# Key-value product folded into the output weight with 32x32 tiles of the TensorE array

## The chip, the cores and the metric

The kernel runs on one core of a Trainium2 chip. The metric is the device time of one execution in microseconds; the time given for a kernel is the median over its runs. TensorE does the matmuls and writes to PSUM, VectorE and ScalarE work element by element and take results out of PSUM, SyncE (SP) issues most of the DMAs. Each engine works through its own queue in order.

## The reference

The whole block is linear attention followed by a token-mixing MLP, both with a pre-LayerNorm and a residual, on 2048 tokens of width 1024. The change touches the attention:

```python
def _A_ref(x, wqkv, wo):
    B, S, D = x.shape
    H = 32; Dh = D // H
    qkv = (x @ wqkv).reshape(B, S, 3, H, Dh)   # then to (3, B, H, S, Dh)
    q, k, v = qkv[0], qkv[1], qkv[2]
    phi = lambda t: jnp.where(t > 0, t + 1, jnp.exp(t)) + 1e-6
    pq, pk = phi(q), phi(k)
    kv = jnp.einsum("bhsd,bhse->bhde", pk, v)
    z = jnp.einsum("bhsd->bhd", pk)
    num = jnp.einsum("bhqd,bhde->bhqe", pq, kv)
    den = jnp.einsum("bhqd,bhd->bhq", pq, z)[..., None] + 1e-6
    o = num / den
    return o.transpose(0, 2, 1, 3).reshape(B, S, D) @ wo
```

There are 32 heads of 32 columns, so `kv` is one 32x32 matrix for each head. Since `num @ wo` is linear in `kv`, a kernel may multiply each head's `kv` into its 32 rows of `wo` first, and then multiply `pq / den` by that product.

## The kernel before

**Stages.** The attention's front end projects K and V, adds up `kv` and the sums of `pk` in PSUM (`kv_ps`, by `kv_accum`), and computes parts of Q in between (`q_fill`). Then comes the stretch that the change lies in, lines 1382 to 1582. After it the output projection runs over 16 blocks of 128 tokens (`seed`, `out_mm`, `out_evac`), and then the MLP, which takes the larger part of the time.

**The stretch around the change.** 128 partitions hold four heads, so the 1024 columns of Q, K, V are eight blocks j of four heads q (`ND` = 8, `HB` = 4, `DH` = 32).

- Lines 1384 to 1392, VectorE: `kv_ps` goes to `kvbd`, one 128x128 block-diagonal matrix for each j, in four instructions (one for each head q of a block, all j at a time). Then `zz` is made of the sums of `pk`. Three units of Q (`q_fill`) run on TensorE meanwhile.
- `kv_transpose`: eight TensorE transposes of `kvbd` into one PSUM bank, one ScalarE copy to `kvT`.
- `load_wo`: `wo` arrives in two DMAs of 1 MB on SP. Its place in SBUF, `wo_sb`, is used for sums of weights by the V projection before (`tv`), so the load waits until that is done. Behind it on SP's queue stand the first MLP weights (`load_w1`, two of 1 MB), four rows of x (`load_xr`), and then the denominators' DMAs.
- A loop of 16 steps n (lines 1567 to 1582). Each step computes one unit of Q with eight matmuls (`q_held`), taken out of PSUM by Exp and Relu on ScalarE and finished by two operations on VectorE. Steps 1 to 8 also run `fold(n - 1)`: two matmuls of 128x128 by 128x512 for block j, one result copied to `wf` (the same place as `wo_sb`, as fp16) by ScalarE, one by VectorE. Steps 0, 2 and 9 run a denominator (`den`): eight matmuls on column tiles of 32, Ln and Exp on ScalarE into `rd_sb`, and a DMA to `rd_dram`; `den_spread` brings it back to all partitions in eight DMAs of 128 KB, each to 32 partitions. `scale_q` multiplies Q by it, `first_sums` prepares MLP weights, both on VectorE.

**Order.** Nearly everything here is held in program order on its engine by `pin` (the helpers `ht`, `hs`, `hv`, `hd` do that; all their instructions carry line 230). The load of `wo` and the `kvbd` pieces are not pinned; a scheduler places them.

**Banks.** [...] `acc_tile` hands out accumulators from a ring of five (two of pool `acc`, three of pool `accx`); the denominators have three (`ndp`). A unit or a fold can start when the bank that it is given has been read out.

Of the kernel before, what the change touches and what calls it, by code (L numbers as in the profile page):

```python
# [10 lines left out]
P = 128  # L11
# [4 lines left out]
ALU = mybir.AluOpType  # L16
PSUM = bass.MemoryType.PSUM
# [4 lines left out]
DH = 32  # L22
# [8 lines left out]
def kernel(  # L31
# [12 lines left out]
    nc = tc.nc  # L44
    x = A_x.flatten_outer_dims()
    o_dram = out.flatten_outer_dims()
    S, D = x.shape
    F = B_w1.shape[1]
    NS, ND, NF = S // P, D // P, F // P
    CW = min(BANK, D)  # L50
    NDC = D // CW
# [7 lines left out]
    HB = P // DH  # L59
# [6 lines left out]
    acc = actx_psum.enter_context(tc.tile_pool(name="acc", bufs=2, space=PSUM))  # L66
    accx = ExitStack()
    acc_ring = [acc]

    def more_acc(bufs):  # L70
        pool = accx.enter_context(tc.tile_pool(name="accx", bufs=bufs, space=PSUM))
        acc_ring[:] = [acc, pool, acc, pool, pool][0:2 + bufs]

    def less_acc():
        accx.close()
# [2 lines left out]
    def acc_tile():  # L78
        acc_ring.append(acc_ring.pop(0))
        return acc_ring[-1].tile([P, BANK], F32, tag="acc", name="acc_t")  # L80

    more_acc(3)

    pin = tc.keep_in_program_order
# [56 lines left out]
    def load_w1(u, half, hold=lambda ins: ins):  # L141
        if half == 0:
            w1_tiles[u] = w_tile(wpool, WLEN)[:, 0:NS * CW].rearrange("p (k f) -> p k f", f=CW)
        k = slice(half * NSP, (half + 1) * NSP)
        hold(nc.sync.dma_start(
            w1_tiles[u][:, k, :],
            B_w1[:, u * CW:(u + 1) * CW].rearrange("(k p) f -> p k f", p=P)[:, k, :],
        ))
# [84 lines left out]
    hv, ht, hs, hd = (Held(e, True) for e in (nc.vector, nc.tensor, nc.scalar, nc.sync))  # L233
# [545 lines left out]
    with ExitStack() as actx:  # L779
# [11 lines left out]
        wo_sb = hstat.tile([P, ND, D], BF16)  # L791
        pqpool = actx.enter_context(tc.tile_pool(name="pqpool", bufs=1))
        pqT = pqpool.tile([P, ND, S], BF16)
        kvbd = pqpool.tile([P, ND, P], BF16)
# [6 lines left out]
        a2k = xctx.enter_context(tc.tile_pool(name="a2k", bufs=4))  # L801

        wqkv_v = A_wqkv.rearrange("(k p) c -> p k c", p=P)
        wo_v = A_wo.rearrange("(k p) c -> p k c", p=P)

        with ExitStack() as a1:
            a1w = a1.enter_context(tc.tile_pool(name="a1w", bufs=1))
# [474 lines left out]
            kv_ps = kvp.tile([P, ND, DH + 1], F32, name="kvps")  # L1282
# [98 lines left out]
                q_fill()  # L1381
            nc.vector.memset(zz[:, :, 0:3 * HB], 0.0)
            nc.vector.memset(zz[:, :, 3 * HB:], float(S))
            for q in range(HB):
                own = slice(q * DH, (q + 1) * DH)
                nc.vector.tensor_scalar(kvbd[own, :, own], kv_ps[own, :, 0:DH], 1.0 / S, None, ALU.mult)
            nc.vector.tensor_tensor(
                zz[:, :, HB:2 * HB],
                kv_ps[:, :, DH:DH + 1].to_broadcast([P, ND, HB]),
# [1 line left out]
                ALU.mult,  # L1391
            )

        more_acc(3)
        warmctx.close()
        kvT = xctx.enter_context(tc.tile_pool(name="kvtpool", bufs=1)).tile([P, ND, P], FP16, name="kvT")
        wpool = sactx.enter_context(tc.tile_pool(name="wpool", bufs=2, side="right"))
        pools["sa"] = mctx.enter_context(tc.tile_pool(name="sapool1", bufs=4, side="right"))

        def load_wo(c):  # L1400
            nc.sync.dma_start(wo_sb[:, :, c * CW:(c + 1) * CW], wo_v[:, :, c * CW:(c + 1) * CW])

        pools["i5"] = mctx.enter_context(tc.tile_pool(name="is0", bufs=1, side="right"))
        pools["is_bufs"] = 4
        a3p = actx.enter_context(ExitStack())
        ndp = a3p.enter_context(tc.tile_pool(name="ndp", bufs=3, space=PSUM))
        rd_dram = [dram.tile([P, SW], FP16, name=f"rd_dram{u}") for u in range(NSC)]

        with ExitStack() as a3:

            def kv_transpose():
                tp = acc_tile()[:].bitcast(BF16).rearrange("p (j f) -> p j f", f=P)
                for j in range(ND):
                    ht.transpose(tp[:, j, :], kvbd[:, j, :], ident[:])
                hs.copy(kvT[:], tp)

            wf = wo_sb[:].bitcast(FP16)

            def fold(j):
                for c in range(NDC):  # L1420
                    cols = slice(c * CW, (c + 1) * CW)
                    ps = acc_tile()
                    ht.matmul(ps[:, 0:CW], lhsT=kvT[:, j, :], rhs=wo_sb[:, j, cols], start=True, stop=True)
                    (hs.copy if c == 0 else hv.tensor_copy)(wf[:, j, cols], ps[:, 0:CW])

            rdbs = {}
            SPREAD = (0, 2, 1, 3)
# [23 lines left out]
            def den_spread(u):  # L1451
                rows = rd_dram[u].rearrange("(g o h) n -> o h g n", g=4, h=HB)
                for h in range(2):
                    rdb = thirds[(2 * SPREAD.index(u) + h) % 3].bitcast(FP16).rearrange("p (j n) -> p j n", n=SW)
                    for q in range(HB):
                        hd.dma_start(
                            rdb[q * DH:(q + 1) * DH, :, :],
                            rows[h, q].unsqueeze(0).to_broadcast([DH, 4, SW]),
                        )
                    rdbs[u, h] = rdb  # L1460

            def den(u):
                den_inv(u, den_mm(u))

            def scale_q(u, h):
                v = pqT[:, h * NH:(h + 1) * NH, u * SW:(u + 1) * SW]
                hv.tensor_tensor(v, v, rdbs.pop((u, h)), ALU.mult)

            def q_held(u, j):
                qp = acc_tile()  # L1470
                for kt in range(ND):
                    ht.matmul(
                        qp[:, 0:SW],
                        lhsT=wq_sb[:, kt, j * P:(j + 1) * P],
                        rhs=xnT[:, kt, u * SW:(u + 1) * SW],
                        start=(kt == 0),
                        stop=(kt == ND - 1),
                    )
                phi_evac(pqT[:, j, u * SW:(u + 1) * SW], qp[:, 0:SW], SW, a2k)
# [14 lines left out]
            def seed(i):  # L1494
                if i < NS:
                    xr = xrs.pop(i)
                    seeds[i] = [acc_tile() for dc in range(NDC)]
                    for dc in range(NDC):
                        hs.copy(seeds[i][dc][:, 0:CW], xr[:, dc * CW:(dc + 1) * CW])
# [40 lines left out]
            def combine_h(q):  # L1540
                combine(hE[:, q, :], hO[:, q, :], hT2[:, q, :], hT3[:, q, :], hT4[:, q, :], hv)

            for c in range(NDC):
                load_wo(c)
            for half in range(2):
                load_w1(0, half, pin)
            for i in range(XRL + 1):
# [2 lines left out]
            def first_sums():  # L1550
                cur = Quad([Mixer1(0), Mixer1(1)])
                for m in (5, 6, 7, 3):
                    yield pin(cur.asums(m))
                cur.in5 = Inner(cur.sts, 5, None, "i5", cur.sink5, cur.sum5)
                Held.on = True
                cur.in5.sums()
                Held.on = False
                yield cur

            for _ in range(2):  # L1560
                acc_ring.append(acc_ring.pop(0))
            sums_at, ahead = (4, 8, 9, 11, 13), first_sums()
            scale_at = {5: (0, 0), 6: (0, 1), 10: (2, 0), 12: (2, 1), 15: (1, 0)}
            den_at = {0: 0, 2: 2, 9: 1}
            spread_at = {0: 0, 6: 2, 12: 1}
            kv_transpose()
            for n, (u, j) in enumerate(q_units[8:]):
                if n == len(q_units) - 8 - 1:
                    seed(0)
                q_held(u, j)  # L1570
                if 1 <= n < 1 + ND:
                    fold(n - 1)
                if n in den_at:
                    den(den_at[n])
                if n in spread_at:
                    den_spread(spread_at[n])
                if n in (12, 13):
                    load_w1(1, n % 2, pin)
                if n in scale_at:
                    scale_q(*scale_at[n])  # L1580
                if n in sums_at:
                    cur = next(ahead)
# [254 lines left out]
```

## Time and profile before

| what | value |
|---|---|
| median of 3 runs | 557.93 us (557.29 to 558.2) |
| the profiled execution | 557.03 us, its span 555.3 us |
| granted TensorE clock | 1.00 throughout |
| fold matmuls (`acc_t<-wo_sb,kvT`) | 16, first at 145.8 us, last at 162.3 us |
| the two DMAs of `wo` | issued at 133.6 and 134.1 us, 5.2 and 7.6 us to landing |
| four `kvbd` pieces on VectorE | from 137.0 us, 0.40 to 0.43 us each |
| transposes of `kvbd` on TensorE | from 141.3 us |
| copies of the folds | eight on ScalarE (0.59 us), eight on VectorE (0.68 us) |
| stretch from the transposes to the end of the 16 units | 141.3 to about 179 us |

Times of single instructions are counted in microseconds from the start of the span. An instruction's length is not its cost: matmuls are pipelined, so a row of eight matmuls of 379 ns each takes 8 x 0.216 us. What counts is the distance from the start of one to the start of the next. A line of the timeline gives the start, the length, the engine, the line of code, the operation with output and inputs, and how often it stands there in a row.

### The profile page before, as it was taken

The numbers are of one execution on the slowest core, as the hardware profiler recorded it, in microseconds if no ns is written. First come the engines' busy times: TensorE is split into PE (matmuls) and PEld (weight loads), VectorE is DVE, ScalarE is ACT, GpSimd is POOL, SyncE is SP. The second block draws the span as 40 slices with busy tenths as digits, with TensorE's granted clock in tenths as the row PEclk, the third lists the DMA queues.
The fourth block names the chain that finished last, engine by engine and source line by source line (L and its number), as shares of the span: only waits on it lengthen the run. The fifth ranks groups of instructions, "written<-read, shape, count | busy, mean of one in ns | idle before, by whom it ended". The sixth has DMA issues, their size and how long they took to land.

```text
span 555.3 us, 9676 instructions
## 1 busy us (share of the span) xinstructions
PE 548.3 (99%) x3754; PEld 316.7 (57%) x3771; DVE 443.6 (80%) x851; ACT 289.0 (52%) x614; POOL 26.2 (5%) x36
## 2 busy tenths in 40 slices
PE   8999999999999999999999999999999999999997
PEld 3444446644444444456666766666444667767665
DVE  7798888755497788889989789887896878749747
ACT  5747678766776877645546465564210412413311
POOL 1000000000000000000000000000003103103111
PEclk9999999999999999999999999999999999999999
DMA  8933341202867951203140440413869649849434
GB/s 295 312 77 77 84 89 20 40 1 97 293 161 209 317 176 76 77 1 109 44 152 15 138 148 6 152 43 90 208 200 238 198 129 244 207 135 237 94 107 75
DMA packets 83934, 74.56 MB, mean 134 GB/s; under 512 B 15650, under 2 KB 76336, under 8 KB 83888
## 3 DMA queue, kind: packets, MB, share of 16 engines
q1 hardware_dynamic: 79504, 69.87, 42.0%
q0 software_dynamic: 4096, 3.68, 4.9%
q8 instruction: 29, 0.48, 0.3%
q10 hardware_dynamic: 288, 0.39, 0.2%
q14 instruction: 17, 0.14, 0.1%
HBM read 59.12 MB, written 11.67 MB: 127 GB/s over the span
## 4 chain that ended last, share of the span: by engine, by line
PE 95%; DMA 2%; ACT 1%; DVE 1%; issue 1%; ACTq 0%; DVEq 0%
PE psI L230 25%; PE psC L230 16%; PE acc_t L230 14%; PE psB L230 8%; PE psC L970 4%; PE psB L970 4%; PE psA L970 4%; PE acc_t L890 3%; PE acc_t L1299 2%; PE psB L342 2%; PE psA L342 2%; PE psE L970 2%; PE psC L342 2%; PE psA L230 1%; PE psE L342 1%; DMA rd_dram<-shared_sb 1%
## 5 line engine op out<-in xcount | busy, mean ns | idle before, releaser
L230 PEld LDWEIGHTS <-is 128*128 128x128 f16 x736 | 71.8, 98 | 31.2 <-DVE hi L230 0.4
L230 PEld LDWEIGHTS <-sa 128*128 128x128 f16 x606 | 59.2, 98 | 27.1
L230 PEld LDWEIGHTS <-wq 128*128 128x128 bf16 (+1 forms) x496 | 48.5, 98 | 28.2 <-issue 1.0
L230 PE MATMUL acc_t<-wo_sb,pqT 128*128 128x512 f16 x256 | 55.6, 379 | 0.0
L487 POOL DMA_DIRECT2D out_dram<-wq x28 | 24.3, 927 | 517.2 <-ACT wq L490 486.9
L230 PEld LDWEIGHTS <-pqT 128*128 128x128 bf16 x256 | 25.0, 98 | 30.5 <-issue 0.6
L230 DVE TENSOR_TENSOR t<-psI,t 128x256 f32<-128x256 f32 (+1 forms) x45 | 20.8, 475 | 22.2 <-PE psI L230 20.9
L190 DVE TENSOR_SCALAR e_sb<-e_sb 128x512 bf16<-128x512 bf16 x64 | 18.4, 288 | 19.7 <-ACT e_sb L185 19.6
L230 PE MATMUL psC<-gs,wq 128*128 128x512 f16 x140 | 34.1, 379 | 0.0
L970 PEld LDWEIGHTS <-xs 128*128 128x128 f16 x208 | 19.7, 98 | 22.3 <-DVE xs L959 0.8
L230 PE MATMUL psC<-hT,sa 128*128 128x512 f16 x112 | 31.2, 379 | 0.0
L230 PE MATMUL psI<-hi,is 128*128 128x256 f16 x200 | 30.0, 273 | 0.0
L230 PE MATMUL psB<-hT,sa 128*128 128x512 f16 x112 | 29.7, 379 | 0.0
L230 PE MATMUL acc_t<-xnT,wq_sb 128*128 128x512 bf16 x125 | 29.3, 379 | 0.3
L230 DVE BATCH_NORM_STATS2 hst<-acc_t 128x6 f32<-128x512 f32 x32 | 21.4, 692 | 9.0 <-ACT h_bf L230 8.9
L185 ACT ACTIVATE e_sb<-acc_t 128x512 bf16<-128x512 f32 x32 | 19.1, 598 | 18.1 <-PE acc_t L1299 9.5
L970 PE MATMUL psA<-wkv,xnT 128*128 128x512 bf16 x96 | 25.9, 379 | 0.4
L970 PEld LDWEIGHTS <-xnT 128*128 128x128 bf16 x156 | 15.2, 98 | 18.7 <-issue 1.1
L230 PE MATMUL psC<-hT,wq 128*128 128x512 f16 x96 | 24.6, 379 | 0.0
L230 ACT CAST h_bf<-acc_t 128x512 bf16<-128x512 f32 x32 | 18.4, 582 | 11.9 <-PE acc_t L230 11.8
L230 DVE TENSOR_TENSOR e<-psI,es 128x256 f32<-128x256 f32 x20 | 8.5, 425 | 19.9 <-PE psI L230 19.9
L230 ACT COPY psI<-psI 128x256 f32<-128x256 f32 x50 | 18.0, 360 | 11.6 <-PE psI L230 9.8
(245 smaller groups left out, 1123.5 us busy)
## 6 DMA issues: line engine op xcount, KB each, us to landing
wq<-in_B_w_dram SPq DMA_DIRECT2D x14, 1024.0 KB, 7.8
wq<-in_B_w_dram SPq DMA_DIRECT2D x12, 896.0 KB, 7.4
gs<-parked SPq DMA_DIRECT2D x9, 896.0 KB, 4.7
shared_sb<-rd_dram SPq DMA_DIRECT2D x32, 128.0 KB, 3.8
out_dram<-h_bf SPq DMA_DIRECT2D x16, 256.0 KB, 2.0
x_sb<-in_A_x_dram SPq DMA_DIRECT2D x14, 256.0 KB, 3.0
w2o<-in_B_w_dram SPq DMA_DIRECT2D x4, 896.0 KB, 11.3
out_dram<-wq POOLq DMA_DIRECT2D x28, 128.0 KB, 4.8
```

The source lines that it names most:

```text
L185: pin(nc.scalar.activation(e_sb[:], src, ACT.Exp))
L190: pin(nc.vector.tensor_scalar(e_sb[:], e_sb[:], 1.0, PHI_EPS, ALU.min, ALU.add))
L230: return (lambda *a, **kw: pin(op(*a, **kw))) if self.always or getattr(Held, self.key) else op
L342: pe.matmul(ps[:, cols], lhsT=lhs[:, k, :], rhs=mv(k)[:, cols], start=(start and k == 0), stop=(k == self.nk - 1), skip_group_check=True,)
L487: nc.gpsimd.dma_start(to, ot[:, a:b], accum_op=ALU.add)
L890: mm = nc.tensor.matmul(pp[:, 0:CW], lhsT=xnT[:, kt, i * P:(i + 1) * P], rhs=wkv[:, kt, c * CW:(c + 1) * CW], start=(kt == 0), stop=(kt == ...
L970: pin(nc.tensor.matmul(ps[:], lhsT=lhs[:, k, :], rhs=rhs[:, k, :], start=(start and k == 0), stop=(k == hk2 - 1), skip_group_check=True,))
L1299: nc.tensor.matmul(qp[:, 0:SW], lhsT=wq_sb[:, kt, j * P:(j + 1) * P], rhs=xnT[:, kt, u * SW:(u + 1) * SW], start=(kt == 0), stop=(kt == ND ...
```

## The change

The product of `kv` and `wo` is computed head by head on 32x32 tiles of the array. A block-diagonal 128x128 matrix would use only the four tiles on the diagonal. So the four blocks of one half (j = 4a + b, b = 0 to 3) are turned against each other: head q of block b sits in rows r = (q + b) mod 4 of its 32-row groups, both in `kvbd` (as columns, before the transposes) and in `wo_sb` (as partitions). Then the 16 heads of the half occupy 16 different tiles (r, q), and a group of 16 matmuls of 32x32 by 32x512 does four blocks for one half of the columns. Tile (r, q) writes partitions of q in the bank of block b.

There are four such groups (two halves by two column halves), in steps 1, 3, 5 and 7, each with two ScalarE and two VectorE copies. `load_wo` becomes 16 DMAs of 128 KB, each to 32 partitions; the `kvbd` pieces become 16. The ring has six banks (four in `accx`) in another order, and the denominators keep two.

```diff
     def more_acc(bufs):
         pool = accx.enter_context(tc.tile_pool(name="accx", bufs=bufs, space=PSUM))
-        acc_ring[:] = [acc, pool, acc, pool, pool][0:2 + bufs]
+        acc_ring[:] = [acc, pool, acc, pool, pool] if bufs == 3 else [pool, pool, pool, acc, acc, pool]
...
-        wo_v = A_wo.rearrange("(k p) c -> p k c", p=P)
+        wo_v = A_wo.rearrange("(a b q e) c -> e a b q c", b=HB, q=HB, e=DH)
+
+        def row_of(q, j):
+            return (q + j) % HB
...
+            turned = kvbd[:].rearrange("p (a b) (r e) -> p a b r e", b=HB, e=DH)
+            sums_v = kv_ps[:, :, 0:DH].rearrange("p (a b) e -> p a b e", b=HB)
             for q in range(HB):
                 own = slice(q * DH, (q + 1) * DH)
-                nc.vector.tensor_scalar(kvbd[own, :, own], kv_ps[own, :, 0:DH], 1.0 / S, None, ALU.mult)
+                for b in range(HB):
+                    nc.vector.tensor_scalar(turned[own, :, b, row_of(q, b), :], sums_v[own, :, b, :], 1.0 / S, None, ALU.mult)
...
-        more_acc(3)
+        more_acc(4)
...
-        def load_wo(c):
-            nc.sync.dma_start(wo_sb[:, :, c * CW:(c + 1) * CW], wo_v[:, :, c * CW:(c + 1) * CW])
+        def load_wo():
+            to = wo_sb[:].rearrange("p (a b) c -> p a b c", b=HB)
+            for q in range(HB):
+                for b in range(HB):
+                    r = row_of(q, b) * DH
+                    nc.sync.dma_start(to[r:r + DH, :, b, :], wo_v[:, :, b, q, :])
...
-        ndp = a3p.enter_context(tc.tile_pool(name="ndp", bufs=3, space=PSUM))
+        ndp = a3p.enter_context(tc.tile_pool(name="ndp", bufs=2, space=PSUM))
...
-            def fold(j):
-                for c in range(NDC):
-                    cols = slice(c * CW, (c + 1) * CW)
-                    ps = acc_tile()
-                    ht.matmul(ps[:, 0:CW], lhsT=kvT[:, j, :], rhs=wo_sb[:, j, cols], start=True, stop=True)
-                    (hs.copy if c == 0 else hv.tensor_copy)(wf[:, j, cols], ps[:, 0:CW])
+            def fold(n):
+                a, c = divmod(n, NDC)
+                cols = slice(c * CW, (c + 1) * CW)
+                ps = [acc_tile() for _ in range(HB)]
+                for r in range(HB):
+                    rows = slice(r * DH, (r + 1) * DH)
+                    for q in range(HB):
+                        b = (r - q) % HB
+                        j, own = a * HB + b, slice(q * DH, (q + 1) * DH)
+                        ht.matmul(
+                            ps[b][own, 0:CW], lhsT=kvT[rows, j, own], rhs=wo_sb[rows, j, cols],
+                            start=True, stop=True, skip_group_check=True, tile_position=(r * DH, q * DH),
+                        )
+                for b in range(HB):
+                    (hs.copy if b % 2 == 0 else hv.tensor_copy)(wf[:, a * HB + b, cols], ps[b][:, 0:CW])
...
-            for c in range(NDC):
-                load_wo(c)
+            load_wo()
...
-            for _ in range(2):
-                acc_ring.append(acc_ring.pop(0))
...
+            fold_at = {1: 0, 3: 1, 5: 2, 7: 3}
...
-                if 1 <= n < 1 + ND:
-                    fold(n - 1)
+                if n in fold_at:
+                    fold(fold_at[n])
```

## The prediction

> **What bounds the kernel now.** First the page's engine table and the engine shares of the chain that ended last:
>
> ```profile
> PE 548.3 (99%) x3754; PEld 316.7 (57%) x3771; DVE 443.6 (80%) x851; ACT 289.0 (52%) x614; POOL 26.2 (5%) x36
> ...
> PE 95%; DMA 2%; ACT 1%; DVE 1%; issue 1%; ACTq 0%; DVEq 0%
> ```
>
> TensorE works almost without a hole, so a matmul saved is time saved, provided that nothing else ends last at that place. The exception is the DMA's 2%. I looked for it in the chain in order of time (start, length, what) around the change:
>
> ```profile
> 144.72 0.57 ACT den_ps L230
> 145.29 0.02 issue
> 145.31 0.61 ACT shared_sb L230
> 145.92 0.02 issue
> 145.94 5.75 DMA rd_dram<-shared_sb
> ...
> 152.26 0.59 ACT e_sb L185
> 152.85 0.49 ACT r_sb L187
> 153.34 0.49 ACT wo_sb L230
> 153.83 0.04 issue
> 153.87 1.24 PE acc_t L230 x5
> ```
>
> ScalarE's Exp of the denominator (`den_inv`) writes `rd_sb`, which a DMA carries to DRAM. That DMA takes 5.75 us and lands at 151.7. The next denominator's Exp needs the same `rd_sb`, so ScalarE, which works in order, stands until 151.7; everything queued behind it (Exp and Relu of unit n=3, then copies of `fold`) is late. What this does to TensorE is in its timeline (start, length, operation; a record is missing here and there):
>
> ```profile
> 135.48 0.67 PE L920 MATMUL kvps<-vaug,pk 128*32 128x33 bf16 x64
> 136.07 5.35 PE L1299 MATMUL acc_t<-xnT,wq_sb 128*128 128x512 bf16 x23
> ...
> 143.53 0.61 PE L230 MATMUL den_ps<-pqT,zz 128*32 128x512 bf16 x8
> 144.08 1.90 PE L230 MATMUL acc_t<-xnT,wq_sb 128*128 128x512 bf16 x7
> ...
> 150.78 0.59 PE L230 MATMUL acc_t<-wo_sb,kvT 128*128 128x512 bf16 x2
> 151.22 1.89 PE L230 MATMUL acc_t<-xnT,wq_sb 128*128 128x512 bf16 x8
> 152.94 0.82 PE L230 MATMUL acc_t<-wo_sb,kvT 128*128 128x512 bf16 x2
> 153.87 1.89 PE L230 MATMUL acc_t<-xnT,wq_sb 128*128 128x512 bf16 x7
> ```
>
> A fold of one j (two matmuls) takes 150.78 to 151.22, 0.44 us; the one at 152.94 takes 0.93. So TensorE loses 0.49 us to that DMA. Why the DMA is slow: it stands behind the 2 MB of `wo`, 2 MB of `w1` and 1 MB of x on one queue. The last fence has the queue's issues, then the load in stretches of 2 us (busy time of PE, PEld, DVE, ACT, POOL, then granted clock, DMA share, GB/s):
>
> ```profile
> 133.63 1.01 SPq L1401 DMA_DIRECT2D wo_sb<-in_A_wo_dram  x2
> ...
> 151.70 3.65 SPq L230 DMA_DIRECT2D shared_sb<-rd_dram  x8
> ```
> ```profile
> 136.00:138.00 2.00, 1.95 (x25) 0.94 (x15) 1.56 (x5) 0.67 (x2) 0.00 (x0) 1.00 1.04 363
> 138.00:140.00 2.00, 2.00 (x11) 0.91 (x10) 1.56 (x5) 1.35 (x3) 0.00 (x0) 1.00 1.08 384
> 140.00:142.00 2.00, 2.00 (x17) 1.18 (x16) 0.72 (x2) 1.36 (x4) 0.00 (x0) 1.00 1.08 381
> ...
> 156.00:158.00 2.00, 2.00 (x11) 0.92 (x10) 1.90 (x4) 1.41 (x4) 0.00 (x0) 1.00 1.00 227
> ```
>
> With 128 partitions at a time the DMA moves 363 to 384 GB/s. In the last line it carries `shared_sb<-rd_dram`, 128 KB to 32 partitions each, and at a full share it moves only 227.
>
> **The folds on the array.** Sixteen matmuls of 512 columns leave, 8 x 0.43 = 3.46 us. Four groups of sixteen 32x32 matmuls come. The trace has no row tiles; the nearest row is the denominator, eight matmuls on four column tiles. From the end of the unit before it (its last matmul starts at 143.22, plus 0.22) to 144.08 it takes 0.64 us for two rounds of four, so one round costs 0.64 - 0.22 = 0.42, the change of tiling on both sides included. A group of 16 that runs in one round has 12 more starts, at 9 ns as in the kvps row (64 in 0.59 us) at most: 0.42 to 0.53, I take 0.50. Four groups: 2.0, a saving of 1.46 us. The other bound: rows of the array take turns, four rounds, 0.42 + 3 x 0.22 and the starts, 1.1 us a group. The outermost: sixteen turns, 0.42 + 15 x 0.22 = 3.7 us. I take one round, since four tiles with four moving operands already overlap in this row.
>
> [...]
>
> **The weight's load.** Two DMAs of 1 MB become sixteen of 128 KB, each to 32 partitions. In the order of the changed program three go first, as soon as the V run's matmuls that read blocks 0, 1, 4, 5 of `wo_sb` are done (the last starts at 129.99, so about 130.4), while the DMA is idle; the other 13 follow from about 133.2. Issue on SP: eight spreads take 3.65 us, 0.46 each, so 13 end at 139.2; behind them stand two `w1` loads, four x rows (0.43 each), done near 142, and the `rd_dram` write, which is not ready before 145.94. The longer issue is hidden by 4 us. Data: now 2.1 MB run from 134.5; summing the stretches, they are through at 140.8. Then 13 x 131 KB = 1.70 MB at 227 GB/s need 7.5 us from 134.4, to 141.9: everything behind on the queue is 1.1 us later. Bound below: if only issue limits, the last is issued at 139.2 and through at 140.4, 0.4 us earlier than now. I take +1.1, because the spread has the same size and the same 32 partitions. Its packets are smaller and its source is one row read 32 times, so the lower end is a real possibility.
>
> [...]
>
> The folds themselves do not wait for `wo`: the first stands at 145.8, landing near 143, cover 2.8 us.
>
> **The wait that decides.** With six banks in the order of the ring, unit n=5 reuses the bank of n=3 (four of six go to each fold). Exp and Relu of n=3 stand behind the blocked Exp. So n=5 can start 1.7 us after the landing (151.7 to the end of Relu, 153.34, and a little). Now n=5 starts at 153.87. Landing now 151.7, after the change 151.7 + 1.1 = 152.8: n=5 starts at 154.5, 0.6 later than now. Without any wait TensorE would come there at 153.87 - 0.49 - 4 x 0.43 + 2 x 0.50 = 152.65, so 1.85 us of standing replace 0.49; the saving of the first two groups is swallowed whole. The last two groups keep theirs: 2 x 0.50 against 4 x 0.43, -0.73. Sum -0.1.
>
> **VectorE.** The four `kvbd` pieces (0.42 us each, 256 elements) become 16 of 64 elements. `zz` has 32 elements and 0.19 us; between the two 0.22 each, 3.6 us instead of 1.7, from 137.04 to 140.6, and 0.7 us of phi operations that the new order puts between them: 141.3. The transposes on TensorE wait for them and start at 141.26, so the 2.5 us of cover are just used up; 0 to 0.2 us late, hidden before n=5 by the 1.85. Bound: 0.42 each gives 144.1, 2.9 us late, and then n=5 starts at 155.5, 1.0 later still, 558.8. Casts out of PSUM stay eight and eight on ScalarE and VectorE, two and two at a time; the second group's last VectorE cast ends some 3.4 us after the landing and the third group starts 3.4 after it (1.7 plus a unit of 1.73), no cover left: +0.1. The denominators' buffers go from three to two; the third denominator comes 18 us after the first's Exp, so nothing.
>
> **Sum.** 0.6 - 0.73 + 0.1 = 0.0; the load's price has more room below (to -0.4) than above, so I write -0.1. It is made against the profiled execution, 557.03 us with a span of 555.3 and 1.7 around it; the median, 557.93, lies 0.9 above, and I carry the difference over to it: 557.8. About 0.2%, 1.1 us, is what a measurement of this kernel can tell from no change.
>
> **The rivals.**
> 1. The weight arrives as fast as it is issued (DMA -0.4). Landing 151.3, n=5 at 153.0: -0.87 - 0.73 = -1.6, 556.3. For it: in 154 to 156 the same spreads still ran at 239 GB/s while partly waiting for issue. Against: 227 at a full share.
> 2. Slower: rows of the array take turns in each group, 1.1 us instead of 0.50. The first two groups still fit ahead of 154.5 (152.65 + 1.2 = 153.85); the last two cost 2.2 against 1.73. 0.6 + 0.47 + 0.1 = +1.2, 559.1; it decides from about 1.05 us a group. Against it: the overlapping denominator; for it: nothing in the trace uses row tiles. This is also the case in which the change does not do what it says.
> 3. The queue is later still: at the longest landing of such a spread, 6.4 us, with eight in flight, 0.8 us each, 13 x 0.8 = 10.4, the landing comes 4.0 later than now, +3.4 from n=5 on, 560.6 in all.
>
> **Chances.** Forecast 0.42 (its own range 556.9 to 558.8), rival 1 0.30, rival 2 0.21, rival 3 0.07. Faster by over 0.2% is rival 1 and an edge of the forecast, 0.32; slower is most of 2, all of 3 and an edge, 0.29; the rest, 0.39, within. The range 555.9 to 559.8 holds rival 1 with its spread and rival 2, and leaves out rival 3 and the edges.
>
> **What would show it.** In the changed profile: a group's 16 matmuls from start to the next unit near 0.5 us (1.1: rival 2); DMA rate 134 to 142 near 220 GB/s or near 280 (rival 1); landing of the first `rd_dram` write near 152.8; TensorE's gap ahead of n=5 near 1.8 us and none elsewhere; the transposes at 141.3. I am wrong if that gap is absent, or if TensorE waits for `kvbd` or for the weight.

## The result, and the profile after

| | before | after |
|---|---|---|
| median, 17 runs each | 557.53 us (556.79 to 558.83) | 561.67 us (557.53 to 565.59) |
| profiled execution, its span | 557.03, 555.3 us | 562.1, 560.2 us |

The ratio, estimated from all runs and not the quotient of the two medians, is 1.0065, with an interval of 1.0046 to 1.0085: slower, and above the range of the prediction. The clearest hint on the page of the changed kernel is its engine table and the engine shares of the chain that ended last:

```profile
PE 550.2 (98%) x3819; PEld 315.6 (56%) x3819; DVE 444.7 (79%) x863; ACT 288.9 (52%) x614; POOL 26.3 (5%) x36
...
PE 91%; DMA 5%; DVE 2%; ACT 1%; SPq 1%; issue 0%; DVEq 0%; ACTq 0%
```

The DMA's share grew from 2% to 5% and VectorE's from 1% to 2%; TensorE's busy time grew too, by 1.9 us, though matmul work was taken out. The first question is where the 4.9 us of span lie. Starts of the same matmuls in both traces give it:

| from, to | before | after | more |
|---|---|---|---|
| span's start to the first fold | 145.82 | 146.06 | 0.24 |
| first fold to first matmul of the output projection | 29.52 | 31.89 | 2.37 |
| to the first `psI<-gi,is` of the second MLP stage | 254.54 | 254.54 | 0 |
| that to TensorE's last matmul | 121.90 | 124.09 | 2.19 |
| to the end | 3.49 | 3.62 | 0.13 |

So there are two places, and the second is 300 us behind the edit. First the changed stretch. The chain in order of time:

```profile
144.30 1.85 PE acc_t L230 x8
...
146.78 7.21 DMA rd_dram<-shared_sb
...
154.58 0.59 ACT e_sb L185
155.17 0.50 ACT r_sb L187
...
155.71 4.35 PE acc_t L230 x26
```

It is the same wait as before, with 7.21 us instead of 5.75, and issued later: it lands at 154.00, 2.3 us after the old 151.69. ScalarE stands for it:

```profile
154.08 0.60 ACT L230 ACTIVATE shared_sb<-den_ps 128x512 f16<-128x512 f32 x1 [4.07 <-DMA rd_dram<-shared_sb]
```

TensorE's timeline shows what hangs on it (in brackets the idle time ahead and who ended it):

```profile
141.42 0.61 PE L230 MATMUL acc_t<-ident,kvbd 128*128 128x128 bf16 x8
...
146.06 0.43 PE L230 MATMUL acc_t<-wo_sb,kvT 32*32 32x512 bf16 x16
146.43 1.90 PE L230 MATMUL acc_t<-xnT,wq_sb 128*128 128x512 bf16 x8
...
151.01 1.90 PE L230 MATMUL acc_t<-xnT,wq_sb 128*128 128x512 bf16 x8
155.71 3.45 PE L230 MATMUL acc_t<-xnT,wq_sb 128*128 128x512 bf16 x8 [2.80 <-ACT r_sb L187]
159.09 0.43 PE L230 MATMUL acc_t<-wo_sb,kvT 32*32 32x512 bf16 x16
```

Sixteen small matmuls take 0.37 us to the next unit, 146.06 to 146.43. The unit at 155.71 (n=5) waits 2.80 us, and then takes 3.4 us where its neighbours take 1.8. The stretches of 2 us explain both (busy time of PE, PEld, DVE, ACT, POOL, then granted clock, DMA share, GB/s):

```profile
134.00:136.00 2.00, 2.00 (x58) 0.95 (x57) 0.43 (x1) 0.86 (x2) 0.00 (x0) 1.00 0.43 132
136.00:138.00 2.00, 2.00 (x43) 1.03 (x34) 1.43 (x8) 0.82 (x2) 0.00 (x0) 1.00 0.47 140
138.00:140.00 2.00, 2.00 (x11) 0.94 (x10) 1.90 (x12) 1.19 (x3) 0.00 (x0) 1.00 0.93 257
...
154.00:156.00 2.00, 0.29 (x1) 0.10 (x1) 0.60 (x2) 1.92 (x5) 0.00 (x0) 0.87 0.27 61
156.00:158.00 2.00, 2.00 (x6) 0.73 (x5) 1.86 (x6) 1.62 (x4) 0.00 (x0) 0.50 0.85 238
158.00:160.00 2.00, 2.00 (x22) 0.59 (x21) 1.39 (x3) 0.81 (x2) 0.00 (x0) 0.78 0.93 221
```

Between 134 and 138 the weight moves at 132 to 140 GB/s with the DMA engines under half busy; before, the line of 136 to 138 had 363. And from 155.5 to 158.9 the granted clock is 0.50. The drop falls into the gap, and it costs another 1.6 us: from n=5 to the next start are 3.38 us, where 146.43 to 148.26 is 1.83. That the gap is its cause is tested below. Last, the queue of SP (start, time to the last issue's end):

```profile
130.12 11.10 SPq L1411 DMA_DIRECT2D wo_sb<-in_A_wo_dram  x16
141.42 1.03 SPq L145 DMA_DIRECT2D wq<-in_B_w_dram  x2
142.49 4.19 SPq L230 DMA_DIRECT2D shared_sb<-in_A_x_dram  x4
146.78 0.36 SPq L230 DMA_DIRECT2D rd_dram<-shared_sb  x1
```

The sixteen issues end at 141.2, the x rows at 146.7. ScalarE has the denominator's Exp done at 146.07, so now the write waits 0.7 us for its turn, where before the x rows were issued 2.7 us ahead of it. What the write stands behind is late as well: the last x row landed at 153.69, 0.3 us ahead of it, and before at 151.32, 0.4 us ahead. So its landing follows the data ahead of it, more than its own turn. Before, w1 and the x rows stood on the queue like this:

```profile
136.27 2.84 SPq L145 DMA_DIRECT2D wq<-in_B_w_dram  x2
139.16 4.06 SPq L230 DMA_DIRECT2D shared_sb<-in_A_x_dram  x4
```

The second place is in the MLP. VectorE's rows of both kernels (the kernel before first), then TensorE's of the changed one:

```profile
469.56 0.62 DVE L230 TENSOR_TENSOR is<-wq 128x896 f16<-128x896 bf16 x1
```
```profile
474.40 0.63 DVE L230 TENSOR_TENSOR is<-wq 128x896 f16<-128x896 bf16 x1 [2.15 <-DMA wq<-in_B_w_dram]
```
```profile
475.75 0.94 PE L230 MATMUL psI<-gi,is 128*128 128x256 f16 x7 [1.62 <-DVE is L230]
```

VectorE stands 2.15 us for a load of `w2` (896 KB to `wq`). It was issued at 463.4; fifteen of its sixteen parts had landed by 471.3, the last one came at 474.4, 3 us behind the others. Before, the same load was issued at 460.8, landed at 469.2, and was wanted at 469.56: 0.36 us of cover. I call this the pause.

### The profile page after: what moved, and what is told of

Read it like the earlier page. It is cut to its first block, busy times and chain, and to the rows that moved or that the text cites. A ratio compares the mean times of both kernels' runs of the same rounds, so it can differ in the third digit from the quotient of the medians.

```text
span 560.2 us, 9816 instructions
## 1 busy us (share of the span) xinstructions
PE 550.2 (98%) x3819; PEld 315.6 (56%) x3819; DVE 444.7 (79%) x863; ACT 288.9 (52%) x614; POOL 26.3 (5%) x36
## 4 chain that ended last, share of the span: by engine, by line
PE 91%; DMA 5%; DVE 2%; ACT 1%; SPq 1%; issue 0%; DVEq 0%; ACTq 0%
PE psI L230 23%; PE acc_t L230 15%; PE psC L230 14%; PE psB L230 8%; PE psC L973 4%; PE psB L973 4%; PE psA L973 4%; PE acc_t L893 3%; PE acc_t L1302 2%; PE psA L342 2%; PE psB L342 2%; PE psE L973 2%; DMA wq<-in_B_w_dram 2%; PE psC L342 2%; DMA wkv<-in_A_wqkv_dram 1%; DMA rd_dram<-shared_sb 1%
## 5 line engine op out<-in xcount | busy, mean ns | idle before, releaser
L230 PE MATMUL acc_t<-xnT,wq_sb 128*128 128x512 bf16 x128 | 30.7, 394 | 2.8 <-ACT r_sb L187 2.8
```

Source lines behind the costliest of these rows:

```text
L230: return (lambda *a, **kw: pin(op(*a, **kw))) if self.always or getattr(Held, self.key) else op
```

## The experiments

All are compared with the kernel before on the same chip (557.7 to 558.0 us). Medians are of 6 to 12 runs, the other two columns of one execution each. They are "fold to output" (29.52 before, 31.89 after) and "MLP" (121.90 and 124.09), the two rows of the table above that moved most.

| kernel | median us | ratio, interval | fold to output | MLP |
|---|---|---|---|---|
| after, `wo` in two DMAs | 557.86 | 1.0002, 0.9989 to 1.0014 | 28.34 | 123.97 |
| before, `wo` in sixteen | 563.39 | 1.0096, 1.0078 to 1.0114 | 33.54 | 123.65 |
| after, second buffer | 558.53 | 1.0000, 0.9981 to 1.0019 | 27.37 | 123.95 |
| after, gap filled | 559.57 | 1.0026, 1.0016 to 1.0036 | 30.81 | 121.90 |
| after, seven DMAs | 557.62 | 0.9986, 0.9971 to 1.0002 | 27.37 | 121.90 |
| after, seven, second buffer | 556.85 | 0.9966, 0.9953 to 0.9980 | 27.37 | 123.62 |
| the same once more | 557.48 | 0.9975, 0.9959 to 0.9992 | 27.37 | 124.28 |
| before, second buffer | 557.23 | 0.9989, 0.9979 to 0.9998 | 29.03 | 122.84 |
| before, shifted | 560.13 | 1.0039, 1.0025 to 1.0053 | 29.57 | 123.98 |
| before, shifted, flat start | 560.07 | 1.0035, 1.0020 to 1.0049 | 29.64 | 123.76 |
| after, seven, buffer, shifted | 558.42 | 1.0010, 0.9999 to 1.0020 | 27.37 | 122.72 |
| the same, flat start | 557.56 | 0.9990, 0.9979 to 1.0001 | 27.37 | 122.60 |

**Is it the load? (two runs)** First the changed kernel with the load of before. It leaves out the turning of `wo`, so its product takes wrong rows, and it stands here for its times alone:

```diff
-            for q in range(HB):
-                for b in range(HB):
-                    r = row_of(q, b) * DH
-                    nc.sync.dma_start(to[r:r + DH, :, b, :], wo_v[:, :, b, q, :])
+            for c in range(NDC):
+                nc.sync.dma_start(wo_sb[:, :, c * CW:(c + 1) * CW], wo_v[:, :, c * CW:(c + 1) * CW])
```

> The changed kernel, but wo loaded as before (two DMAs of 1 MB, rows not turned, so the product takes the wrong rows of wo). Theory A (the sixteen DMAs to 32 partitions delay the rd_dram write behind them; TensorE stands about 3 us ahead of unit n=5 and its clock is then halved for 3.4 us): the write lands near 151.7 instead of 154.0, the gap ahead of n=5 falls from 3.0 to about 0.8 us, granted clock 1.00, and the groups' saving comes through: 556.2, 1.3 below the kernel before. Rival B (the tile groups, six banks or sixteen kvbd pieces cost the time): stays near 561.

Its chain, then its TensorE:

```profile
145.76 5.92 DMA rd_dram<-shared_sb
```
```profile
153.40 1.89 PE L230 MATMUL acc_t<-xnT,wq_sb 128*128 128x512 bf16 x8 [0.82 <-ACT r_sb L187]
```

The landing is back at 151.7, the gap is 0.82 us, and the clock stays at 1.00 there. Fold to output is 1.18 us shorter than before. Yet the median is 557.86: the MLP row took 2.1 us back, in a pause at 509.9 in this profile.

Then the kernel before with sixteen DMAs to 32 partitions each, rows not turned, everything else old (the loop above, with `r = q * DH`):

> The kernel before, with nothing changed but the load of wo in sixteen DMAs of 128 KB to 32 partitions (rows in their old places). Theory A: the rd_dram write lands near 154, TensorE stands 2.3 us longer than before and the clock drops as in the changed kernel: 557.5 + 2.3 + 1.7 = 561.5. Rival B: the load alone costs nothing, 557.5.

Its chain and its TensorE, then its clock (second number from the right is the DMA share, before it the clock):

```profile
146.81 8.01 DMA rd_dram<-shared_sb
```
```profile
156.53 0.58 PE L230 MATMUL acc_t<-wo_sb,kvT 128*128 128x512 bf16 x1 [2.67 <-ACT r_sb L187]
```
```profile
158.00:160.00 2.00, 1.78 (x6) 0.65 (x5) 2.00 (x3) 0.43 (x1) 0.00 (x0) 0.52 0.83 223
```

The load alone, with the old folds, gives the late landing (154.82), the gap, the halved clock and 4.0 us more from fold to output. Of the 5.7 us by which the median grew, another 1.7 lie in the MLP row. Turning the rows is not needed for it, and the small tiles are not either.

**Is it the one buffer, and is it the clock? (two runs)** A second `rd` tile for u == 2 leaves the load late but lets nobody wait for it:

```diff
-                hs.activation(rd_sb, ps[:], ACT.Exp, scale=-1.0)
-                hd.dma_start(rd_dram[u][:], rd_sb)
+                rd = rd_two[:] if u == 2 else rd_sb
+                hs.activation(rd, ps[:], ACT.Exp, scale=-1.0)
+                hd.dma_start(rd_dram[u][:], rd)
```

> The changed kernel with a second buffer for the denominator of n=2, so that its Exp needn't wait for the first rd_dram write. Theory A: no gap ahead of n=5, clock 1.00, whole saving of the groups (1.7) and the 0.5 that the kernel before loses there: 555.6. Rival C (without that wait the next one takes its place: VectorE's casts or the second write): between 556.5 and 558. Rival B: near 561.

TensorE runs through the place (the third group at 154.36 instead of 159.09):

```profile
150.80 3.63 PE L230 MATMUL acc_t<-xnT,wq_sb 128*128 128x512 bf16 x15
154.36 0.43 PE L230 MATMUL acc_t<-wo_sb,kvT 32*32 32x512 bf16 x16
```

Fold to output is 27.37, 4.52 less than in the changed kernel. The lowest run, 555.25, is near the 555.6 that was expected of the kernel; the median, 558.53, is not, and the MLP row is 2.05 longer than before.

The next one leaves the wait and gives TensorE idle work in it, whose result nobody reads:

```diff
+                if n == 5:
+                    idle = ndp.tile([P, SW], F32, tag="den", name="den_ps")
+                    for t in range(14):
+                        ht.matmul(idle[:], lhsT=wq_sb[:, 0, 0:P], rhs=xnT[:, 0, 0:SW], start=True, stop=True)
```

> The changed kernel with 14 idle matmuls (3.0 us, into a free denominator bank) ahead of unit n=5, where TensorE stands. The wait stays, the idling goes. Theory A: n=5 starts where it did (155.7), its eight matmuls take 1.7 us instead of 3.5, clock 1.00, 1.7 below the changed kernel: 560.0. Rival D (the slow matmuls after the gap are not caused by idling): no gain or, with the 3 us of matmuls, a loss: 561.7 or more.

```profile
152.56 3.19 PE L230 MATMUL den_ps<-xnT,wq_sb 128*128 128x512 bf16 x14
156.00 1.89 PE L230 MATMUL acc_t<-xnT,wq_sb 128*128 128x512 bf16 x8 [0.25 <-ACT r_sb L187]
```
```profile
156.00:158.00 2.00, 2.00 (x24) 0.81 (x23) 1.87 (x5) 1.98 (x5) 0.00 (x0) 1.00 0.72 207
```

Unit n=5 starts even later (156.00), but takes 1.89 us instead of 3.45, at a granted clock of 1.00 instead of 0.50. Fold to output becomes 1.08 us shorter by useless work. That separates the two costs: the wait, and the clock that the wait costs. It holds beyond the profiles: the mean clock is 0.997 or less in 14 of 17 executions of the changed kernel and in 4 of 6 of the kernel before with sixteen DMAs, and 0.999 or more in all 12 with the gap filled. The two of those six that kept their clock took 561.4 us, the other four 563.3 or more. The median falls by 2.1; the other half of that is not shown to come from the clock, since in this profile the MLP row has no pause either.

**A load that is turned but wide.** A block b only has to be turned by 32 b partitions, so it takes one DMA for b = 0 and two for each other, seven in all:

```diff
+            for b in range(HB):
+                at = b * DH
+                nc.sync.dma_start(to[at:P, :, b, :], wo_v[0:P - at, :, b, :])
+                if b:
+                    nc.sync.dma_start(to[0:at, :, b, :], wo_v[P - at:P, :, b, :])
```

> The changed kernel with wo in seven wider DMAs (block 0 of each half to all 128 partitions, the turned blocks in pieces of 96+32, 64+64 and 32+96 partitions; the same bytes to the same places as the sixteen). Theory A (it is the sixteen DMAs to 32 partitions that make the denominator's DMA late): wo is through near 141.5, the first rd_dram write lands at 151.7 to 152.5 instead of 154.0, TensorE stands 0.8 to 1.5 us ahead of unit n=5 and its clock is not lowered there. Without a pause in the MLP's second stage that gives 556.3; with the pauses that the kernel with two DMAs showed (557.86), 558.0. Rival (what counts is that a turned load can't run at full rate at all): landing 153 or later, the clock lowered, 560.5 or more.

SP's queue, then TensorE:

```profile
136.69 1.01 SPq L145 DMA_DIRECT2D wq<-in_B_w_dram  x2
137.75 4.44 SPq L230 DMA_DIRECT2D shared_sb<-in_A_x_dram  x4
145.79 0.33 SPq L230 DMA_DIRECT2D rd_dram<-shared_sb  x1
150.66 3.94 SPq L230 DMA_DIRECT2D shared_sb<-rd_dram  x8
```
```profile
150.71 3.63 PE L230 MATMUL acc_t<-xnT,wq_sb 128*128 128x512 bf16 x15
154.26 0.43 PE L230 MATMUL acc_t<-wo_sb,kvT 32*32 32x512 bf16 x16
```

The spread that waits for the write is issued at 150.66: the landing is 1.0 us earlier than in the kernel before, probably because three of the seven, half of the bytes, go from 129.8 while the DMA is idle (of the sixteen, three carried 384 KB by then). No gap is left, even with the one buffer. The rival, that a turned load must be slow, falls. The profiled run, which has no pause, takes 555.06 us; the median, 557.62, again lies higher.

> The changed kernel with the seven wider DMAs and a second buffer for the second denominator, so that neither the landing nor the Exp can stop TensorE. No gap ahead of n=5, clock 1.00. Front part as in the run with the second buffer alone. If the pause of the MLP's second stage (VectorE waiting for a w2 load) comes as often as there: 558.4, with single runs at 555.3; if the pause had to do with the narrow load: 555.5.

> The changed kernel with seven wider DMAs and the second buffer, once more, beside its shifted copy: 556.9, lowest 555.05, if the earlier 12 runs speak for it; up to 558.4 if they were lucky.

Two sets of 12 runs, medians 556.85 and 557.48, lowest 555.05 and 555.08: this is the fastest version, 0.25 to 0.34% below the kernel before. That the second buffer adds to it is not shown: fold to output is 27.37 with it and without, and the intervals of the three ratios overlap.

**The old wait.** The second buffer in the kernel before:

> The kernel before with a second buffer for the second denominator, so that its Exp waits for no DMA. It measures the old wait alone: TensorE's instructions do not move against each other, so the fetches fall as before. Prediction's reading (0.49 us): 557.2 to 557.3 against 557.7, the fold at 152.94 followed after 0.44 us instead of 0.93.

Fold to output falls from 29.52 to 29.03, by 0.49 us, the time from 558.0 to 557.23.

**The pause.** In the runs that have no long gap (two DMAs, second buffer, seven DMAs) some executions come out as the stretch says (555.1 to 556.1) and most some 2 us higher. What could the edit change at 470 us? The trace has a DMA queue of the kind `instruction` in pieces of 16 KB, about 1 us each, one every 12 to 28 us, 29 before and 30 after. I take it for the queue that fetches TensorE's instructions; by the pages that would be 63 bytes before and 64 after for each of the 7525 and 7638 matmuls and weight loads, an estimate from the two counts, and no run shows whose they are. The change has 96 TensorE instructions more (64 matmuls with their weight loads instead of 16), so if it is, all later fetches fall at other places. I moved them on purpose, in both directions, with small matmuls at the start:

```diff
             warm_up(1, ln[0][6][:])
+            for t in range(48):
+                pin(nc.tensor.matmul(warm_tiles[t % 5][0:2, 0:2], lhsT=warm[:, 0:2], rhs=warm[:, 0:2], start=True, stop=True))
```

(80 in the changed kernel with seven DMAs and the second buffer.)

> The kernel before with 48 matmuls of two columns added to TensorE's idle time near 6 us: 96 instructions, as many as the change adds. Theory F: its fetches move to where the changed kernel has them, VectorE waits for a w2 load once or twice between 465 and 515 us in most runs, median 559.3, lowest 557. Rival (the pause has another cause): 557.7, as the kernel before.

> The kernel with seven DMAs and the second buffer, and 80 matmuls of two columns added to TensorE's idle time near 6 us (160 instructions with their weight loads). Theory F: TensorE's instructions come in DMAs of 16 KB, and the changed kernel has 96 more of them, so that such a fetch now falls at 457 to 462 us, 1.5 us before a w2 load is issued, and delays one DMA engine's share of it, where before it fell at 468.4, after the load. 160 more move the fetches to near the old places: no pause of VectorE for wq between 465 and 515, median 555.6. Rival (the pause does not depend on where fetches fall): as the kernel without the 80, near 558.4.

These cost something at the start (the first fold came 0.9 us late in the one, 2.2 in the other, where the clock was lowered for 3.4 us near 8 us). So I repeated both with part of the warming-up matmuls left out in exchange:

> The kernel before with TensorE's instruction count raised by 96, as the change raises it, but without the 0.95 us that the 48 small matmuls cost at the start: 51 of two columns stand among the warming-up matmuls, three of which (512 columns) are left out in exchange. K and V projections start within 0.2 us of the kernel before. Theory F (where the 16 KB instruction fetches fall decides how often a w2 load comes too late): the single runs stand 1.5 to 2.5 us above the lowest of the kernel before, median 558.9, with a fetch near 460 and the pause of VectorE for wq near 470. Rival (the start's delay made the difference): 557.8, as the kernel before.

> The changed kernel with seven wider DMAs, the second buffer, and 160 more TensorE instructions, 85 matmuls of two columns among the warming-up matmuls in exchange for five of those, so that the start is no later and the fetches fall where the kernel before has them (469 and 507). Theory F: median 1.0 us above its lowest, as in the kernel before: 556.1, below the kernel without the shift. Rival: the same as that kernel, 556.9 or, if the pauses are as in the run with sixteen DMAs, 558.4.

The starts weren't flat: 0.85 and 1.6 us later than in the profiles of the unshifted kernels (of which others start up to 1.0 late by themselves). Hence the medians missed their numbers. The MLP rows do not depend on the start. Sorted by where a fetch falls against the issue of the first of the two critical `w2` loads (the second follows 39 to 42 us later):

| fetch falls | kernels | MLP, us over 121.90 |
|---|---|---|
| 1.2 to 1.7 us ahead of the load | after; second buffer; two DMAs; seven; seven with buffer, twice; before shifted, twice | 2.2; 2.1; 2.1; 0.0; 1.7; 2.4; 2.1; 1.9 |
| 4.9 us ahead | gap filled | 0.0 |
| 7.4 to 8.1 us behind | before; before with buffer; seven with buffer shifted, twice | 0.0; 0.9; 0.8; 0.7 |
| 7.4 behind, and 2.7 behind the second load | before, sixteen DMAs | 1.8 |

VectorE's row in the shifted kernel before (flat start), with the old folds and the old load:

```profile
472.42 0.63 DVE L234 TENSOR_TENSOR is<-wq 128x896 f16<-128x896 bf16 x1 [1.82 <-DMA wq<-in_B_w_dram]
```

Shown: with 96 more instructions the kernel before has the pause in both profiles and lost 2.1 us, of which at most 0.9 lies at the start; with 160 more, the pause of the kernel with seven DMAs and the second buffer went from 1.7 and 2.4 us to 0.8 and 0.7. Not shown: that the fetch itself holds up the load. A fetch takes about 1 us, and the late part of the load came 3 us after the others; its last packets run beside the output's writes from POOL's queue (`out_dram<-wq`), two of which, landing at 472.92 and 473.91, had one late part too, 0.8 and 1.1 us behind the other fifteen. It is one profile for each kernel, seven DMAs ran without a pause at the bad place, with two DMAs the pause came at the second load, and the kernel before with sixteen DMAs has a pause of 1.7 us with no TensorE instruction added. An earlier start of the load, the direct cure, was not tried.

TensorE itself does not show a late fetch: among its listed waits (0.2 us and more) in the profiles of before, after, two DMAs, sixteen in the kernel before, second buffer and gap filled, those of the MLP, up to 1.62 us, end with VectorE or ScalarE. Whether a fetch can hold up another engine's tightly timed load is what stays open here.

## Why the prediction was wrong, point by point

- **The folds** (0.50 us a group, 1.46 saved): right. From 29.03 to 27.37, both without the wait, 1.66 us are saved, 0.45 a group. One round, so the second rival (rows in turn, 1.1 us) falls. Four row tiles shared each bank, and 16 matmuls were through in 0.37 us.
- **kvbd and the weight**: transposes forecast for 141.3, found at 141.42, and no wait for either (`wo` was in at 144.18, 1.9 us ahead of the first group). Right, in part by luck: the `kvbd` pieces follow each other after 0.14 us, not 0.22, and the last three stand among more of Q's operations than forecast, until 140.73.
- **The chain from landing to TensorE** (n=5 starts 1.7 us after the landing; 152.65 without a wait; the last two groups keep their gain): 154.00 to 155.71 is 1.71; with seven DMAs n=5 comes 1.73 after 150.71, at 152.44; both late groups take 0.37. Right, and the old wait of 0.49 was measured as 0.49. The 0.1 for VectorE's casts does not show.
- **The load's price** is the first term that was mis-sized: +1.1 us on the landing, measured 2.31. I took 227 GB/s from the spreads for all 13 late DMAs. From 138 on they ran at 257 and 252, but from 134 to 138 at 132 to 140, as one issue of them took 1.86 us and the DMA ran half dry meanwhile. After that an issue each 0.47 us set the pace at least as much as the data: the fourth of the sixteen landed 3.57 us after its issue and the last 3.39, so nothing piled up behind it, but the last was issued at 140.79 and through at 144.18, where the forecast had the issue's end at 139.2. The same paragraph held that the longer issue is "hidden by 4 us". It wasn't: w1 and the x rows were issued behind it until 146.7. That sum took 0.43 us for each x row, 1.7 in all, where the queue of before already shows 4.06: one x row in it took 2.63 us and one load of w1 2.43. Why single issues take so long no run here shows. The third rival had the direction (0.8 us a DMA, landing 4.0 later, 560.6) and got 0.07.
- **The price of standing** is the step that failed. I charged a wait of TensorE by its length, "1.85 us of standing replace 0.49". The sum has no term for the clock. At 2.80 us of standing it fell to 0.50 for 3.41 us, and unit n=5 cost 1.55 us more. By lengths alone fold to output would be 27.37 + 2.80 = 30.17, 0.65 over before; it is 31.89. Filling the gap gave 1.08 us of it back, though the filling ended 0.3 us late. Term by term in the profiled stretch, against a forecast of 0.6 - 0.73 + 0.1: n=5 came 1.60 us later after the first fold than before, the clock cost 1.55, and the rest of the stretch is 0.78 shorter; together 2.37.
- **What I did not look at**: the rest of the kernel was taken as unchanged. The MLP load with 0.36 us of cover was to be seen in the trace of before. It makes 2.19 us of the profiled difference; what makes that load late stays open. For the medians it is about what is left: 4.14 less 2.37 is 1.8, if the stretch took in most runs what it took in the profile (in three of the 17 the clock was 1.00 throughout, and these are among the fastest five).

The clock was at 0.50 for 3.41 us with the gaps of 2.80 us (changed kernel) and 2.67 us (sixteen DMAs in the kernel before), and stayed at 1.00 with one of 0.82 us (two DMAs) and with the one of 1.62 us ahead of 475.75 in the changed kernel; nothing between 1.62 and 2.67 was measured. The place of a gap may count beside its length: in the traces of the two kernels the clock's full-speed stretches, each of which ends in a drop, are whole multiples of 3.41 us long (552.96 us, 162 of them, before; 150.19 and 402.77 us, 44 and 118, after), and in three of 17 executions of the changed kernel and two of the six with sixteen DMAs it did not fall. No run here moved the gap alone. For rival 3, with a gap near 4.7 us by its own numbers (157.4 less 152.65), I would now add a term of about the 1.6 us that n=5 lost here; that is an estimate, as no gap of that length ahead of further matmuls was measured.

## What to carry to other kernels

A weight whose rows are permuted should be loaded in the widest pieces that the permutation allows; here seven pieces instead of sixteen took away the loss of 4 us, and with a second buffer the kernel was 0.3% faster than before. A wait of TensorE is not priced by its length alone: waits of 2.67 and 2.80 us came here with 3.41 us at half the clock, so add such a stretch to a wait of that length, and ask what lies on the same queue behind the added issues. And when an edit changes the number of instructions, look through the whole trace for loads that land just in time, since these may turn late far away from the edit.

## What was not expected of the hardware

With gaps of 2.67 and 2.80 us the granted clock was at 0.50 for 3.41 us in the profiles, and with 14 useless matmuls in the gap it was at 1.00 and the median 2.1 us lower. Sixteen 32x32 matmuls of 512 columns, four row tiles to a bank, ran in 0.37 us. And with 48 matmuls of two columns added at the very start, a kernel got a wait of 2.05 us, until 472.66, that it did not have.
